# Seven instead of six quads of a first MLP product as seven half-size products, with relus one addition later

## The chip, the cores and the metric

The kernel runs on one core of a Trainium2 chip. The metric is the device time of one execution in microseconds (us); lower is better. Three runs of the kernel before were timed, and one further execution was profiled.

## The reference, cut to what matters

Block-sparse attention, and behind it a token-mixing and a channel-mixing MLP with residuals:

```python
x  = softmax(masked(q @ k.T / 8)) @ v            # 4 batches, 8 heads, 768 tokens, 64 columns a head
a1 = alpha1 * x + beta1
u  = x + lam * einsum('ts,bsd->btd', w_tok, a1)  # 768 x 768 over the tokens
a2 = alpha2 * u + beta2
ch = maximum(a2 @ w_ch1, 0.0) @ w_ch2            # 512 -> 2048 -> 512
out = u + lam * ch
```

The change lies in `a2 @ w_ch1` of the last batch, batch 3.

## The kernel before

The kernel writes out the order of its work by hand. The first batches' attention is laid out by a table of due times; from then on strings of letters (`W1`, `W2`, `W2L`, `W3`) say which job comes next. A letter takes one job from a list: `f` a job of the first MLP product, `g` one of the second, `S` a sum on VectorE that prepares the second product, `W` a sum of weights for the first, `D` a difference of the first product's inputs. The order of the jobs in the strings is the order in which each engine gets its instructions; each engine works through its own in that order and waits by semaphores. The four strings of `W3` are the end of the kernel, when the attention is nearly done: the third and fourth of them hold nothing but `f`, `S` and `g`.

The hidden layer of 2048 is cut into 16 rows of 128, and the 768 tokens into two halves of 384. A *direct job* (`job_f1`, lines 915 to 927) computes one row for one half of the tokens: four matmuls of 384 columns (L919) over the input's four blocks of 128, accumulated in one bank of PSUM, then a relu on ScalarE (L926) that writes `hts` in bf16.

A *quad* is rows n and n + 8 for both halves: four direct jobs, 16 matmuls. In batch 3 a quad can be done instead by seven products of half the depth (Strassen's scheme in Winograd's form), each two matmuls: 14. This is `job_m(n, m)`, product m of quad n, matmuls at L1016. Products 1, 6, 5 and 3 add up in one bank (of tag `sp` or `op`), products 7 and 4 in another, product 2 is alone (both tag `mm`, which has three banks and is also used by the direct jobs). After products 1, 6 and 5 ScalarE copies the partial sum out (`keep_sum`, L999); after 3 it writes the relu (L1027). After products 2, 7 and 4 VectorE adds the kept partial sum to the bank (L1032) and, in a second instruction, takes the maximum with zero (L1035). Product 4 adds into the bank of product 7, after VectorE's addition has read it. So a quad costs VectorE three additions and three relus.

The products take sums of weight blocks (`job_w`, L974, tile `wsum`, for all quads at once) and differences of the inputs (`job_d`, L989). Before, quads 0 to 5 are done this way (`FS = 6`) and the eight direct jobs of quads 6 and 7 stand between them: `last_f1` gives product m of quad n the place 7n + (0, 4, 6, 8, 10, 12, 16) for m = 1, 6, 2, 5, 7, 3, 4, and puts direct jobs at places 1, 5, 42, 46, 48 and 50; two come at the end.

The second MLP product of batch 3 is done by seven products too (`job_p`, matmuls at L1170, additions at L1180, 256 columns each). Its inputs X1, X2 and two differences are the `S` jobs (`job_s`, L1144): 128x512 for half of the rows, 128x1024 for the last of each three. They read the rows that the relus write. The first job of the second product needs rows 0 to 7 of the first half of the tokens, the second one rows 8 to 15.

Of the kernel before, what the change touches and what calls it, by code (L numbers as in the profile page):

```python
# [13 lines left out]
BF = mybir.dt.bfloat16  # L14
# [6 lines left out]
S = 768  # L21
D = 64
# [4 lines left out]
P = 128  # L27
# [53 lines left out]
]  # L81
W3 = [
# [4 lines left out]
]  # L87
STR = (2, 3)
HN = NH // 2
HC = DM // 2  # L90
FS = 6
WEAVE = W1 + W2 + W2L + W3
ENG = {
    "kT0": 0,
# [154 lines left out]
def kernel(  # L249
# [16 lines left out]
    nc = tc.nc  # L266
# [22 lines left out]
    ap_ = ctx.enter_context(tc.tile_pool(name="attn", bufs=1))  # L289
# [4 lines left out]
    def ptile(shape, dt, name):  # L294
        return pp.tile(shape, dt, name=name, tag=name)
# [72 lines left out]
    for n, src in enumerate((moe_lam, moe_alpha1, moe_beta1)):  # L368
# [10 lines left out]
        out=identb[:],  # L379
# [33 lines left out]
    for o in (slice(0, 4), slice(4, NT)):  # L413
# [4 lines left out]
        out=eqt,  # L418
        in0=sampi[0:NBLK, 0 : 2 * NR : 2]
        .unsqueeze(2)  # L420
        .broadcast_to([NBLK, NR, NBLK]),
        in1=eqt,
        op=ALU.is_equal,
# [8 lines left out]
        out=mbs[0:NBLK, :],  # L432
        in0=mbm[0:NBLK, :],
        scalar1=1.0,
# [26 lines left out]
    def sp_tile():  # L461
        return psum.tile([P, 2, 512], FP, name="sp", tag="sp", bufs=2)
# [6 lines left out]
    def mm_tile(shape=(P, DM), dt=FP):  # L469
        return psum.tile(list(shape), dt, name="mm", tag="mm", bufs=3)  # L470

    def op_tile(shape):
        phase["op"] += 1
        if phase["first"] and phase["op"] % 2 == 0:
            return mm_tile(shape)
        return psum.tile(shape, FP, name="op", tag="op", bufs=1)
# [246 lines left out]
    rest = ptile([P, P], FP, "rest")  # L723
# [85 lines left out]
    did = set()  # L809
# [101 lines left out]
    def h_row(b, c, n):  # L911
        if (b, c) not in hts:
            hts[(b, c)] = ap_.tile([P, NH, QC], BF, name="hts", tag="hts", bufs=2)
        return hts[(b, c)][:, n, :]
# [14 lines left out]
    wsum, usum = [], []  # L929
# [19 lines left out]
        7: (3, 3),  # L949
    }  # L950

    def w_of(name, ks, n=slice(0, FS)):
        if isinstance(name, int):
            return wsum[0][:, name - 1, ks, n.start * P : n.stop * P]
        r, c = int(name[0]) - 1, int(name[1]) - 1
        at = slice((HN * r + n.start) * P, (HN * r + n.stop) * P)
        return w1b[:, 2 * c + ks.start : 2 * c + ks.stop, at]

    def u_of(name, ks):
        if isinstance(name, int):  # L960
            t = usum[0][:, name - 1].rearrange("p (k c) -> p k c", k=2)
            return t[:, ks]
        r, c = int(name[0]) - 1, int(name[1]) - 1
        return uTs[B - 1][:, 2 * r + ks.start : 2 * r + ks.stop, ts(c, QC)]

    def job_w(n, ks):
        if not wsum:
            wsum.append(
                ap_.tile([P, 4, 2, FS * P], BF, name="wsum", tag="x_sb", bufs=3)
            )  # L970
        a, b, op = WSUM[n]
        for name in (a, b):
            assert isinstance(name, str) or ("W", name, ks.start) in did
        nc.vector.tensor_tensor(  # L974
            out=w_of(n, ks), in0=w_of(a, ks), in1=w_of(b, ks), op=op
        )
        did.update(("W", n, k) for k in range(ks.start, ks.stop))

    def job_d(n, ks):
        if not usum:  # L980
            usum.append(ap_.tile([P, 4, S], BF, name="uT", tag="uT", bufs=2))
        a, b, op = USUM[n]
        for name in (a, b):
            for k in range(ks.start, ks.stop):
                if isinstance(name, int):
                    assert ("D", name, k) in did
                else:
                    assert ("u", 2 * int(name[0]) - 2 + k) in did
        nc.vector.tensor_tensor(  # L989
            out=u_of(n, ks), in0=u_of(a, ks), in1=u_of(b, ks), op=op  # L990
        )
        did.update(("D", n, k) for k in range(ks.start, ks.stop))
# [3 lines left out]
    def keep_sum(n, name):  # L996
        tag = {1: "kr", 6: ("a1pp128", "ubf")[n % 2], 5: "vr"}[name]
        t = ap_.tile([P, QC], FP, name="part", tag=tag, bufs=2)
        nc.scalar.copy(t[:], chain[(n, 1)][:, 0:QC])  # L999
        chain[(n, "s", name)] = t  # L1000

    def job_m(n, m):
        b = B - 1
        if m == 1 and n % 3 < 2:
            chain[(n, 1)] = sp_tile()[:, 0]
        elif m == 1:
            chain[(n, 1)] = op_tile([P, DM])[:]
        elif m in (2, 7):
            chain[(n, m)] = mm_tile()[:]
        ps = chain[(n, {2: 2, 7: 7, 4: 7}.get(m, 1))]  # L1010
        w, u = PROD1[m]
        for k in range(2):
            ks = slice(k, k + 1)
            assert isinstance(w, str) or ("W", w, k) in did
            assert isinstance(u, str) or ("D", u, k) in did
            nc.tensor.matmul(  # L1016
                ps[:, 0:QC],
                w_of(w, ks, slice(n, n + 1))[:, 0],
                u_of(u, ks)[:, 0],
                start=(m in (1, 2, 7) and k == 0),  # L1020
                stop=(k == 1),
                skip_group_check=True,
            )
        if m in (1, 6, 5):
            keep_sum(n, m)
        elif m == 3:
            nc.scalar.activation(h_row(b, 1, n), ps[:, 0:QC], AF.Relu)  # L1027
            did.add(("f", b, 1, n))
        else:
            part, c, row = {2: (1, 0, n), 7: (5, 1, HN + n), 4: (6, 0, HN + n)}[m]  # L1030
            h = h_row(b, c, row)
            nc.vector.tensor_tensor(  # L1032
                out=h, in0=ps[:, 0:QC], in1=chain[(n, "s", part)][:], op=ALU.add
            )
            nc.vector.tensor_scalar_max(out=h, in0=h, scalar1=0.0)  # L1035
            did.add(("f", b, c, row))

    def last_f1():
        at = {1: 0, 6: 4, 2: 6, 5: 8, 7: 10, 3: 12, 4: 16}
        slot = {7 * n + k: (n, m) for n in range(FS) for m, k in at.items()}  # L1040
        rest = [(c, r + n) for c in range(2) for n in range(FS, HN) for r in (0, HN)]
        jobs = []
        for k in range(max(slot) + 1):
            if k in slot:
                jobs.append(slot[k])
            elif rest and k in (1, 5, 42, 46, 48, 50):
                jobs.append((B - 1,) + rest.pop(0))
        return jobs + [(B - 1,) + j for j in rest]

# [63 lines left out]
    xs = {}  # L1113

    def a_of(b, t, name, r=slice(0, HN)):
        if name in ("X1", "X2"):
            return xs[(b, t, name)][:, r]
        c, half = {"11": (0, 0), "12": (0, 1), "21": (1, 0), "22": (1, 1)}[name]
        return hts[(b, c)][:, HN * half + r.start : HN * half + r.stop, ts(t, P)]
# [7 lines left out]

    def job_s(b, t, n, r=slice(0, HN)):
        dst, a, c, op = SOP[n]
        rows = range(r.start, r.stop)  # L1130
        for name in (a, c):
            if name[0] == "X":
                assert all(("S", b, t, int(name[1]), m) in did for m in rows)
            else:
                h, half = divmod(int(name) - 11, 10)
                assert all(("f", b, h, HN * half + m) in did for m in rows)
        if n == 3:
            assert all(("S", b, t, 1, m) in did for m in rows)
        if n == 4:
            assert (b, t, 2) in did  # L1140
        if dst[0] == "X" and (b, t, dst) not in xs:
            tag, bufs = ("eT", 6) if b == B - 1 else ("xs", 4)
            xs[(b, t, dst)] = ap_.tile([P, HN, P], BF, name="xs", tag=tag, bufs=bufs)
        nc.vector.tensor_tensor(  # L1144
            out=a_of(b, t, dst, r), in0=a_of(b, t, a, r), in1=a_of(b, t, c, r), op=op
        )
        did.update(("S", b, t, n, m) for m in rows)
# [116 lines left out]
    todo = {"f": [], "g": [], "t": [], "S": []}  # L1264
# [52 lines left out]
    for m in (32, 64):  # L1317
        nc.gpsimd.tensor_tensor(
            out=pick[0:96],
            in0=identb[0:96, 0:12] if m == 32 else pick[0:96],  # L1320
            in1=identb[0:96, m : m + 12],
            op=ALU.add,
# [137 lines left out]
    def token(t, p):  # L1460
# [31 lines left out]
            todo[t].pop(0)()  # L1492

    halves = [slice(0, 1), slice(1, 2)]
    todo["W"] = [lambda n=n, k=k: job_w(n, k) for n in (1, 3, 2, 4) for k in halves]
    todo["D"] = [lambda: job_d(1, slice(0, 2))] + [
        lambda n=n, k=k: job_d(n, k) for k in halves[::-1] for n in (2, 3, 4)
    ]
    todo["A"] = [lambda t=t, n=n: job_t(*t, n) for t in T_ORDER for n in range(0, HN, 2)]
# [32 lines left out]
```

## Time and profile before

| | |
|---|---|
| median of 3 runs | 298.61 us (298.60 to 298.87) |
| the profiled execution | 298.76 us, span 297.1 us |
| TensorE matmul (PE), share of the span | 98% |
| VectorE (DVE) | 80% |
| ScalarE (ACT) | 73% |
| first matmul of batch 3's seven products | at 255.34 us |
| first matmul of its second product | at 274.91 us |

In rows of the timeline the first number is the start in us from the span's start, the second the duration; then follow engine, line, operation, what is written and read, the shape, and how many instructions are merged in the row. A merged row's duration is from the start of its first to the end of its last. A bracket at the end gives the idle time before it and what ended it. PE is TensorE, PEld its weight load. A row of the chain of waits has start, duration, engine, tile and line. In the table of stretches each engine has its busy us and, in brackets, its instructions, and the granted clock follows.

### The profile page before, as it was taken

What the parts mean: (1) busy time and instruction counts of PE and PEld (TensorE: products, weight loads), DVE (VectorE), ACT (ScalarE), POOL (GpSimd) and SP (SyncE); (2) the same over time, 40 slices, a digit from 0 to 9 for tenths busy, and PEclk for the clock granted to TensorE, in tenths of its full rate; (3) what the DMA queues carried; (4) which work ended last, traced back from release to release, by engine and by line L of the source; (5) the groups of instructions that cost most, each with busy time, mean ns of one, the idle gap of its engine ahead of it and who ended that gap; (6) DMA issues with size and microseconds to landing.
All of it is one profiled execution on the core that took longest, in us unless ns stands there. A gap on an engine that the chain in (4) does not pass through costs nothing.

```text
span 297.1 us, 7554 instructions
## 1 busy us (share of the span) xinstructions
PE 289.7 (98%) x3082; PEld 193.5 (65%) x3101; DVE 237.8 (80%) x485; ACT 217.1 (73%) x324; POOL 109.8 (37%) x149
## 2 busy tenths in 40 slices
PE   8999999999999999999999999999999999999995
PEld 3688888665567565565576466556576679665884
DVE  4988899995678796977878777895956899799774
ACT  4999999998899963999779581999869744576000
POOL 8997978632443710355323340335320300000000
PEclk9999999999999999999999999999999999999999
DMA  6999999992392995729955767745520211400032
GB/s 182 184 199 186 192 171 187 171 123 44 95 147 55 112 203 84 118 65 119 125 96 73 124 110 146 103 92 69 70 62 17 38 38 29 141 1 3 0 141 73
DMA packets 57274, 31.09 MB, mean 105 GB/s; under 512 B 37204, under 2 KB 54016, under 8 KB 57240
## 3 DMA queue, kind: packets, MB, share of 16 engines
q0 software_dynamic: 16752, 14.22, 34.4%
q1 hardware_dynamic: 40020, 15.92, 29.3%
q8 instruction: 24, 0.39, 0.6%
q10 hardware_dynamic: 468, 0.47, 0.5%
q14 instruction: 10, 0.08, 0.1%
HBM read 29.75 MB, written 6.29 MB: 121 GB/s over the span
## 4 chain that ended last, share of the span: by engine, by line
PE 84%; DVE 6%; DMA 4%; ACT 3%; issue 1%; POOL 1%; SPq 0%; POOLq 0%
PE mm L919 18%; PE mm L1058 13%; PE sp L601 10%; PE mm L846 8%; PE op L671 7%; PE mm L1170 5%; PE sp L1170 4%; PE mm L601 3%; DVE eT L636 3%; PE mm L822 3%; PE op L648 2%; DMA vr<-in_v_dram 2%; ACT eT L619 2%; PE mm L1016 2%; PE sp L1016 2%; DMA uraw<-ubf 2%
## 5 line engine op out<-in xcount | busy, mean ns | idle before, releaser
L619 ACT ACTIVATE eT<-sp,expb 128x1024 f16<-128x1024 f32 x111 | 118.4, 1120 | 2.1 <-PE sp L601 1.4
L636 DVE TENSOR_TENSOR eT<-eT,mask 128x1024 f16<-128x1024 f16 x99 | 80.6, 843 | 13.5 <-ACT eT L619 13.3
L919 PE MATMUL mm<-uT,w1b 128*128 128x384 bf16 x416 | 76.8, 326 | 0.4 <-ACT hts L926 0.3
L705 POOL TENSOR_TENSOR a1pp<-x_sb,vbc 128x384 bf16<-128x384 f32 x25 | 28.5, 1138 | 119.0 <-DVE x_sb L689 84.7
L619 ACT ACTIVATE eT<-mm,expb 128x512 f16<-128x512 f32 x66 | 41.7, 685 | 26.5 <-PE mm L601 26.3
L926 ACT ACTIVATE hts<-mm 128x384 bf16<-128x384 f32 x104 | 49.1, 502 | 13.3 <-PE mm L919 12.4
L919 PEld LDWEIGHTS <-w1b 128*128 128x128 bf16 x416 | 38.7, 98 | 26.4 <-issue 2.9
L1058 PE MATMUL mm<-w2b,hts 128*128 128x512 bf16 x205 | 52.2, 379 | 0.9 <-issue 0.2
L671 PEld LDWEIGHTS <-eT 128*128 128x128 f16 x792 | 29.8, 98 | 8.8 <-issue 1.7
L1058 PEld LDWEIGHTS <-hts 128*128 128x128 bf16 x224 | 19.8, 98 | 22.3 <-issue 3.9
L671 PE MATMUL op<-vext,eT 128*128 128x65 f16 x792 | 32.1, 194 | 0.4 <-DVE x_sb L689 0.3
L601 PE MATMUL sp<-qTs,kTs 88*128 88x512 bf16 (+1 forms) x120 | 26.9, 325 | 1.2 <-ACT eT L619 0.7
L706 POOL TENSOR_TENSOR a1pp<-a1pp,vbc 128x384 bf16<-128x384 bf16 x25 | 26.7, 1069 | 2.0
L846 PE MATMUL mm<-a1pp,wtokT 128*128 128x256 bf16 x216 | 25.9, 273 | 0.1
L846 PEld LDWEIGHTS <-wtokT 128*128 128x128 bf16 x216 | 20.6, 98 | 5.6 <-issue 1.8
L1170 PEld LDWEIGHTS <-hts 128*128 128x128 bf16 x208 | 19.5, 98 | 3.0 <-issue 0.3
L858 DVE TENSOR_TENSOR x_sb<-x_sb,mm 128x512 f32<-128x512 f32 x18 | 12.3, 686 | 9.9 <-PE mm L846 9.8
L601 PE MATMUL sp<-qhT,khT 64*128 64x256 bf16 (+1 forms) x176 | 19.8, 322 | 0.0
L601 PEld LDWEIGHTS <-khT 64*128 64x128 bf16 x264 | 10.6, 94 | 12.7 <-issue 9.2
L648 PEld LDWEIGHTS <-eT 128*128 128x128 f16 x360 | 14.9, 97 | 3.8 <-issue 0.3
L689 DVE TENSOR_TENSOR x_sb<-op,rcp 128x384 f32<-128x384 f32 x28 | 15.6, 558 | 1.0
L1067 DVE TENSOR_TENSOR x_sb<-x_sb,mm 128x512 f32<-128x512 f32 x14 | 9.6, 686 | 8.2 <-PE mm L1058 6.7
(135 smaller groups left out, 376.9 us busy)
## 6 DMA issues: line engine op xcount, KB each, us to landing
out_dram<-x_sb SPq DMA_DIRECT2D x23, 256.0 KB
qpad<-in_q_dram POOLq DMA_DIRECT2D x15, 192.0 KB, 4.6
kr<-in_k_dram POOLq DMA_DIRECT2D x15, 192.0 KB, 5.3
vr<-in_v_dram POOLq DMA_DIRECT2D x15, 192.0 KB, 6.3
w1b<-in_moe_w_ch_dram POOLq DMA_DIRECT2D x4, 512.0 KB, 9.2
w2b<-in_moe_w_ch_dram POOLq DMA_DIRECT2D x4, 512.0 KB, 7.7
hts<-in_moe_w_tok_dram POOLq DMA_DIRECT2D x2, 576.0 KB, 8.7
x_sb<-in_k_dram ACTq DMA_DIRECT2D x2, 192.0 KB
```

Of the source, the lines that this page charges most:

```text
L601: nc.tensor.matmul(sp[jj][:, dst], lhsT, rhs, start=True, stop=True, skip_group_check=True,)
L619: nc.scalar.activation(dst, at, AF.Exp, bias=expb[:], scale=SCALE)
L636: nc.vector.tensor_mul(out=e, in0=e, in1=keep)
L648: nc.tensor.matmul(op[0][:, o, :], ets[u][:, jj, h * QB + n * P : h * QB + n * P + P], vexts[i % NVB][:, w, 2 * jp + jj, :], start=op[1] == 0,
L671: nc.tensor.matmul(op[0][:, o, :], ets[u][:, jj, h * QB + n * P : h * QB + n * P + P], vexts[i % NVB][:, w, 2 * jp + jj, :], start=op[1] == 0,
L705: eng.tensor_tensor(out=dst, in0=x_sbs[b][:, :, cols], in1=bc[0], op=ALU.mult)
L706: eng.tensor_tensor(out=dst, in0=dst, in1=bc[1], op=ALU.add)
L846: nc.tensor.matmul(ps[:, o], wtokT[:, os_, ts(2 * n + o, P)], a1pps[i][:, os_, :], start=(os_ == 0 and o == 0), stop=(os_ == NT - 1 and o ...
L919: nc.tensor.matmul(ps[:, 0:QC], w1b[:, dk, ts(n, P)], uTs[b][:, dk, ts(c, QC)], start=(dk == 0), stop=(dk == 3),)
L926: nc.scalar.activation(h_row(b, c, n), ps[:, 0:QC], AF.Relu)
L1058: nc.tensor.matmul(ps[:], ht[:, nk, ts(o % 3, P)], w2b[:, nk, :], start=(nk == 0), stop=(nk == NH - 1),)
L1170: nc.tensor.matmul(ps, a_of(b, t, a)[:, r], b_rows(m, r)[:, 0, cols], start=(start and r == 0), stop=(r == HN - 1), skip_group_check=True,)
```

## The change

`FS` becomes 7: quad 6 is done by seven products too, and only quad 7 has direct jobs. The weight sums of quad 6 have a tile of their own from the pool of tag `xs`; they are four instructions more (128x256), and four letters `W` at the end of the first string of `W3` place them behind the last differences `D`. In the third string three `f` are added and the `S` are placed anew. Direct jobs stand at places 1, 5, 49 and 53. VectorE's relu after a product is not issued behind its own addition but behind the next one (`raw`, `relu_late`); an `S` job issues it first if it is still due.

```diff
 W3 = [
-    "a p p p g s g g T S T S T S S S d g g U g v g D g D D g D g D g D D",
+    "a p p p g s g g T S T S T S S S d g g U g v g D g D D g D g D g D D W W W W",
     "f f f f f f f f f f f f f f f f f f f f f",
-    "f f f f f f f f f f f f f f f S f f S f f f S S f f S f f S S f f S f f f S f",
+    "f f f f f f f f f f f f f f f f f f S f f S f f S f f S f S f f S f S f f S f f S",
     "S S g S g S g g g S S g S g S g g g S S g S g g g g g S g g g g g",
 ]
-FS = 6
+FS = 7
+FW = 6
...
-    def w_of(name, ks, n=slice(0, FS)):
+    def w_of(name, ks, n):
         if isinstance(name, int):
-            return wsum[0][:, name - 1, ks, n.start * P : n.stop * P]
+            at = n.start // FW
+            return wsum[at][:, name - 1, ks, (n.start - FW * at) * P : (n.stop - FW * at) * P]
...
-    def job_w(n, ks):
-        if not wsum:
-            wsum.append(
-                ap_.tile([P, 4, 2, FS * P], BF, name="wsum", tag="x_sb", bufs=3)
-            )
+    def job_w(n, ks, cs):
+        at = cs.start // FW
+        if len(wsum) == at:
+            tag, bufs = (("x_sb", 3), ("xs", 4))[at]
+            shape = [P, 4, 2, (cs.stop - cs.start) * P]
+            wsum.append(ap_.tile(shape, BF, name="wsum", tag=tag, bufs=bufs))
...
+    raw = []
+
+    def relu_late():
+        while raw:
+            h, name = raw.pop()
+            nc.vector.tensor_scalar_max(out=h, in0=h, scalar1=0.0)
+            did.add(name)
+
...
             nc.vector.tensor_tensor(
                 out=h, in0=ps[:, 0:QC], in1=chain[(n, "s", part)][:], op=ALU.add
             )
-            nc.vector.tensor_scalar_max(out=h, in0=h, scalar1=0.0)
-            did.add(("f", b, c, row))
+            relu_late()
+            raw.append((h, ("f", b, c, row)))
...
-            elif rest and k in (1, 5, 42, 46, 48, 50):
+            elif rest and k in (1, 5, 49, 53):
...
     def job_s(b, t, n, r=slice(0, HN)):
         dst, a, c, op = SOP[n]
+        relu_late()
...
-    todo["W"] = [lambda n=n, k=k: job_w(n, k) for n in (1, 3, 2, 4) for k in halves]
+    both = slice(0, 2)
+    todo["W"] = [
+        lambda n=n, k=k: job_w(n, k, slice(0, FW)) for n in (1, 3, 2, 4) for k in halves
+    ] + [lambda n=n: job_w(n, both, slice(FW, FS)) for n in (1, 3, 2, 4)]
```

In the order that results, TensorE has two matmuls fewer, and all jobs up to place 41 of `last_f1` stand as before, but that the first two direct jobs are now of quad 7. From there on TensorE's jobs are 6.1, 5.5, 4.4, 5.7, 6.6, 5.3, 6.2, a direct job, 6.5, 5.4, 6.7, a direct job, 6.3 and 6.4, where 6.4 is product 4 of quad 6.

More of the change, by code (lines that the diff above doesn't have):

```diff
@@ L964, in u_of @@
         return uTs[B - 1][:, 2 * r + ks.start : 2 * r + ks.stop, ts(c, QC)]
-    def job_w(n, ks):
-        if not wsum:
-            wsum.append(
-                ap_.tile([P, 4, 2, FS * P], BF, name="wsum", tag="x_sb", bufs=3)
-            )
+    def job_w(n, ks, cs):
[4 more added lines that the diff above has]
+            wsum.append(ap_.tile(shape, BF, name="wsum", tag=tag, bufs=bufs))
         a, b, op = WSUM[n]
         for name in (a, b):
-            assert isinstance(name, str) or ("W", name, ks.start) in did
+            for k in range(ks.start, ks.stop):
+                assert isinstance(name, str) or ("W", name, k, at) in did
         nc.vector.tensor_tensor(
-            out=w_of(n, ks), in0=w_of(a, ks), in1=w_of(b, ks), op=op
+            out=w_of(n, ks, cs), in0=w_of(a, ks, cs), in1=w_of(b, ks, cs), op=op
         )
-        did.update(("W", n, k) for k in range(ks.start, ks.stop))
+        did.update(("W", n, k, at) for k in range(ks.start, ks.stop))
     def job_d(n, ks):
@@ L1013, in job_m @@
             ks = slice(k, k + 1)
-            assert isinstance(w, str) or ("W", w, k) in did
+            assert isinstance(w, str) or ("W", w, k, n // FW) in did
             assert isinstance(u, str) or ("D", u, k) in did
@@ L1494 @@
     halves = [slice(0, 1), slice(1, 2)]
-    todo["W"] = [lambda n=n, k=k: job_w(n, k) for n in (1, 3, 2, 4) for k in halves]
-    todo["D"] = [lambda: job_d(1, slice(0, 2))] + [
+    both = slice(0, 2)
+    todo["W"] = [
+        lambda n=n, k=k: job_w(n, k, slice(0, FW)) for n in (1, 3, 2, 4) for k in halves
+    ] + [lambda n=n: job_w(n, both, slice(FW, FS)) for n in (1, 3, 2, 4)]
+    todo["D"] = [lambda: job_d(1, both)] + [
         lambda n=n, k=k: job_d(n, k) for k in halves[::-1] for n in (2, 3, 4)
```

1 row of the table W3 is left out of this document.

## The prediction

> **What bounds the kernel now.** I read the page first, then the busy time by stretches, then the timeline of the stretch that the change touches, then the chain that ended last.
>
> ```profile
> span 297.1 us, 7554 instructions
> PE 289.7 (98%) x3082; PEld 193.5 (65%) x3101; DVE 237.8 (80%) x485; ACT 217.1 (73%) x324; POOL 109.8 (37%) x149
> core 0: us, PE busy (x) PEld busy (x) DVE busy (x) ACT busy (x) POOL busy (x), PEclk, DMA share, GB/s
> 260.00:270.00 10.00, 10.00 (x63) 6.00 (x62) 9.46 (x27) 7.40 (x18) 0.00 (x0) 1.00 0.01 2
> ```
>
> The page says that TensorE bounds the whole: 98%. The stretch from 260 to 270 us, in the middle of batch 3's first product, says something narrower. TensorE is full, at a granted clock of 1.00, but VectorE is busy for 9.46 of 10 us. A change that trades matmuls for VectorE work there spends what hardly exists. I write 6.4 for product 4 of quad 6. The timeline gives the pace of both engines:
>
> ```profile
> 260.95 0.56 DVE L1032 TENSOR_TENSOR hts<-mm,part 128x384 bf16<-128x384 f32 x1
> 261.54 0.26 DVE L1035 TENSOR_SCALAR hts<-hts 128x384 bf16<-128x384 bf16 x1
> 261.72 0.55 DVE L1032 TENSOR_TENSOR hts<-mm,part 128x384 bf16<-128x384 f32 x1
> ...
> 262.05 0.49 PE L1016 MATMUL sp<-uT,w1b 128*128 128x384 bf16 x2
> 264.32 0.49 PE L1016 MATMUL sp<-uT,w1b 128*128 128x384 bf16 x2
> ```
>
> The two TensorE rows are 3.1 and 4.1, the first products of two quads that follow each other: 14 matmuls in 2.27 us, 0.162 each. The VectorE rows are an addition, its relu 0.59 us later (0.03 after the addition ended, so it waited for it), and the next addition 0.18 after that (0.08 before the relu ended, since those two are independent). One addition and its relu so cost 0.76 us, three of them per quad 2.28. The two engines are level: 2.27 against 2.28. What then ended the time of TensorE at the stage's end:
>
> ```profile
> 270.01 0.74 PE mm L1016 x4
> 270.75 0.67 PE mm L919 x4
> 271.45 0.50 ACT hts L926
> 271.99 1.46 PE mm L919 x8
> ...
> 271.25 0.49 PE L1016 MATMUL op<-uT,wsum 128*128 128x384 bf16 x2
> ```
>
> The chain leaves TensorE once: a direct job waited for ScalarE's relu to free its bank, 0.42 us (by the timeline's last row the two matmuls in front began at 271.25, so its own could have followed at 271.57, and began at 271.99; the relu ended at 271.95, so a bank is passed on in about 0.05). After that TensorE runs without a pause into the second product.
>
> **The change part by part.** *TensorE.* Quad 6's four direct jobs are 16 matmuls of 384 columns, its seven products are 14: two fewer, 2 x 0.162 = 0.32 us, if TensorE stays the bound. The 0.42 us wait goes too, since that direct job is gone. ScalarE loses four relus of direct jobs and gains three copies of partial sums and one relu: as many instructions of about the same size, on an engine that is busy for 7.40 of 10 us; I cost it at nothing.
>
> *The four weight sums (128x256).* They stand on VectorE between the last difference of u and the first addition.
>
> ```profile
> 255.88 0.62 DVE L989 TENSOR_TENSOR uT<-uT 128x384 bf16<-128x384 bf16 x2
> 257.96 0.56 DVE L1032 TENSOR_TENSOR hts<-mm,part 128x384 bf16<-128x384 f32 x1 [1.46 <-PE mm L1016]
> ...
> 252.72 1.04 PE L1170 MATMUL sp<-qTs,xs 128*128 128x256 bf16 x8
> ```
>
> VectorE is idle there for 1.46 us, from 256.50 to 257.96. No row has this size: half of the pair of 128x384 is 0.31, a 128x512 of the same kind 0.42 (below), a whole relu 0.26. I take 0.26, nearest to smaller work; four are 1.0 us and fit. At 0.42 they are 1.7 and delay the first addition by 0.2, which VectorE makes up in the next quads, where it will have time over. Their buffer, one of the four of xs, has no reader left: the last matmuls on an X1 or X2 of batch 2 are those of 252.72. Cost at the end: none by either bound.
>
> *Each relu one addition later.* Between additions the relu no longer waits for the addition before it. A following independent instruction starts 0.08 before the end of the one in front, and that holds for work out of PSUM too:
>
> ```profile
> 252.04 0.42 DVE L1180 TENSOR_TENSOR x_sb<-x_sb,sp 128x256 f32<-128x256 f32 x1
> 252.38 0.55 DVE L989 TENSOR_TENSOR uT<-uT 128x768 bf16<-128x768 bf16 x1
> ```
>
> 0.34 us from start to start for a duration of 0.42. So an addition followed by somebody else's relu takes 0.555 - 0.08 = 0.475, against 0.59 now, and the pair 0.475 + 0.18 = 0.655; three per quad are 1.97 us, 0.3 under TensorE's 2.27. In quads 0 to 3 this saves nothing, because TensorE sets their pace. And the relu is flushed at every sum that prepares the second product (L1144): where such a sum comes right after an addition, the relu follows its own addition as before.
>
> *The end of the stage.* This decides. The sums of L1144 must come out of VectorE in this stage too:
>
> ```profile
> L1032 DVE TENSOR_TENSOR hts<-mm,part 128x384 bf16<-128x384 f32 x18 | 9.9, 552 | 1.9 <-PE mm L1016 1.5 <-ACT part L999 0.3
> L1035 DVE TENSOR_SCALAR hts<-hts 128x384 bf16<-128x384 bf16 x18 | 4.7, 260 | 0.6
> L1144 DVE TENSOR_TENSOR xs<-xs,hts 128x512 bf16<-128x512 bf16 x3 | 1.3, 418 | 0.0
> ...
> 269.15 0.26 DVE L1035 TENSOR_SCALAR hts<-hts 128x384 bf16<-128x384 bf16 x1
> 269.32 0.75 DVE L1144 TENSOR_TENSOR xs<-hts 128x512 bf16<-128x512 bf16 x2
> 270.00 0.55 DVE L1032 TENSOR_TENSOR hts<-mm,part 128x384 bf16<-128x384 f32 x1
> ```
>
> Two sums take 0.68 to the next addition, 0.34 each. Before, six direct jobs stand at the end of the stage: 24 matmuls, 3.9 us of TensorE that ask nothing of VectorE. Now there are two, and three additions with three relus more. The order of the changed kernel on VectorE from addition 3.4 on is: 3.4, relu, 4.7, relu, 5.2, two relus, two sums, 4.4, 5.7, two relus, two sums, 6.2, its relu, two sums, 5.4, its relu, a sum, 6.7, its relu, a sum, 6.4, its relu. Up to 3.4 the jobs of TensorE are the same as before, so the matmuls of 3.4 stay where they are:
>
> ```profile
> 267.25 0.49 PE L1016 MATMUL mm<-uT,w1b 128*128 128x384 bf16 x2
> ...
> 274.91 1.04 PE L1170 MATMUL sp<-w2b,hts 128*128 128x256 bf16 x8
> 275.78 1.04 PE L1170 MATMUL mm<-w2b,hts 128*128 128x256 bf16 x8
> ```
>
> They end at 267.74 and the addition starts at about 267.77. From there VectorE does not pause: five additions followed by something independent, 5 x 0.475 = 2.38; four followed by their own relu (6.2, 5.4, 6.7, 6.4), 4 x 0.58 = 2.32; nine relus at 0.18 = 1.62; eight sums at 0.34 = 2.72. Together 9.04: the relu of 6.4 starts at 276.81 and ends at 277.07.
>
> TensorE meets this queue twice. Product 4 of a quad adds into the bank of product 7, so 6.4 waits until addition 6.7 has read it. Counted back from 276.81, addition 6.7 runs from 275.13 to 275.68, and 6.4's matmuls start near 275.7. Unhindered they would start near 273.9 (274.91 less the 0.42, less 0.32 saved, less their own 0.32): new idle time of about 1.8 us, most of it in one piece ahead of 6.4, behind which the whole second product is queued. The next product but one (the second with 256 columns, 275.78 before) reads row 14 of the first half, which the relu of 6.4 writes; it starts at 277.07 + 0.05 = 277.12. That is 277.12 - 275.78 = **+1.34 us**. The saved 0.32 and the vanished 0.42 are inside this, used up by the wait. From there the second product keeps its order and TensorE its pace; its sums come on VectorE 1.3 us later, as all of it does.
>
> The profiled execution took 298.76 us, 1.66 more than its span, and the median is 298.61, so I add to the median: 298.61 + 1.34 = **299.9 us**.
>
> **The rivals.** *The late relus bring nothing.* The rows speak against it (0.75 for two independent sums of 0.42 each). If an addition holds the engine for 0.58 whatever follows, VectorE is behind from the fourth addition on, as it is now: 260.95 + 17 x 0.76 + 8 x 0.34 = 276.59 for addition 6.4, its relu ends at 277.43, the second product goes on at 277.48: +1.70, 300.3 us. The Trainium skill, page "VectorE: DVE Perf Modes", section "The DRAIN you can't avoid", states this as a rule: the next operation does not start until the pipe is empty, and chaining without semaphores does not skip it; it adds that an operation that isn't held starts earlier. The overlap of 0.08 in the rows is on the side of that addition.
>
> *TensorE stays the bound.* Then VectorE would have to finish the relu of 6.4 about 2.1 us earlier than I count: the second product would start 0.32 + 0.42 = 0.74 earlier, near 274.2, and the time is 297.9, or 298.3 if only the matmuls are saved. For it speaks that TensorE is 98% busy and that quads 0 to 3 gain a slack of 0.3 us each on VectorE. Against it: that slack comes before the sums may start, so it cannot be used for them. The point from which it decides is the sum of 9.04 us being under about 7.0.
>
> *In between.* If the nine additions, nine relus and eight sums each cost 0.03 us less than taken, the wait shrinks by 0.8 and the time is 299.2; at 0.05 less it is 298.6, no change.
>
> **How the numbers follow.** About 0.2%, 0.6 us, is what a measurement of this kernel can tell from no change. VectorE as the new bound with late relus at +1.34: 0.77. The same without their help, +1.70: 0.12. In between and within 0.6 us: 0.05. TensorE still the bound, faster: 0.06. So slower 0.89, same 0.05, faster 0.06. The range goes from 299.2 (each term 0.03 us less) to 300.5 (the first rival and 0.2 for terms that are larger than taken).
>
> **What would show it.** In the profile after: a TensorE pause of about 1.5 us or more ahead of the last product 4, with a VectorE addition as the releaser, and VectorE without idle time from about 268 to 277 us. The first product of the second stage starts about 1.1 us later than 274.91. Additions in quads 1 to 3 have relus of the job before right behind them, 0.475 later, and idle time after them. The four weight sums lie inside 256.4 to 257.9. I am wrong if TensorE has no pause over 0.5 us there, or if VectorE shows idle time after 268.

## The result, and the profile after

| | before | after |
|---|---|---|
| median | 298.69 us (19 runs, 298.21 to 299.14) | 299.54 us (19 runs, 299.02 to 300.77) |
| profiled execution | 298.76 us, span 297.1 | 300.77 us, span 299.0 |

The changed kernel is slower: the ratio is 1.003, with an interval of 1.0022 to 1.0038, or 0.85 us from median to median (0.7 to 1.1 by the interval). 299.9 was forecast, with a range of 299.2 to 300.5.

The profiled execution of after is the slowest of its 19 runs. Part of its surplus lies ahead of the change: batch 3's first product begins at 256.29 us, and at 255.34 before, although the instructions up to there are the same in the same order; the other traces of this study begin between 255.00 and 255.87. So I do not compare times on the scales of two traces, but the time from that first matmul. First the page of after:

```profile
span 299.0 us, 7563 instructions
PE 290.0 (97%) x3080; PEld 193.2 (65%) x3099; DVE 240.1 (80%) x495; ACT 217.0 (73%) x324; POOL 109.7 (37%) x149
```

Two matmuls fewer (their weight loads, PEld, go from 3101 to 3099; the PE counts of these two traces lack some 19 records each, which other traces have), ten VectorE instructions more (four weight sums, three additions, three relus), as many on ScalarE. TensorE's share falls although its work hardly shrinks: it waits. Where is shown by TensorE's timeline of after, from the start of the stage to the second product:

```profile
256.29 0.49 PE L1028 MATMUL sp<-uT,w1b 128*128 128x384 bf16 x2
...
273.07 0.49 PE L1028 MATMUL mm<-uT,w1b 128*128 128x384 bf16 x2
273.49 0.48 PE L1028 MATMUL mm<-uT,wsum 128*128 128x384 bf16 x2
274.04 0.81 PE L920 MATMUL mm<-uT,w1b 128*128 128x384 bf16 x4
274.69 0.49 PE L1028 MATMUL sp<-uT,wsum 128*128 128x384 bf16 x2
276.56 0.48 PE L1028 MATMUL mm<-uT,w1b 128*128 128x384 bf16 x2 [1.39 <-DVE hts L1044]
276.89 1.03 PE L1183 MATMUL sp<-w2b,hts 128*128 128x256 bf16 x8
277.76 1.04 PE L1183 MATMUL mm<-w2b,hts 128*128 128x256 bf16 x8
```

The last product of the last quad, 6.4, waits 1.39 us after the end of 6.3, with VectorE's addition (L1044 now) as the releaser. From the stage's first matmul to the second product's first it took 274.91 - 255.34 = 19.57 us before, and 276.89 - 256.29 = 20.60 now: +1.03. From there to the last addition of the kernel both take 18.66 us (293.57 - 274.91 and 295.55 - 276.89). The whole difference is in this stage. It can be added up from start to start, with two matmuls at 0.32: 1.55 us are lost ahead of 6.4 (6.3 begins at 274.69), 0.22 ahead of the direct job at 274.04 and 0.09 ahead of 6.7 (273.49), together 1.86. Before lost 0.42 there and another 0.08 (269.85 to 270.26 for two matmuls). With the two matmuls saved, 1.86 - 0.50 - 0.32 = 1.04. What 6.4 waits for, on VectorE:

```profile
268.72 0.56 DVE L1044 TENSOR_TENSOR hts<-mm,part 128x384 bf16<-128x384 f32 x1 [0.25 <-PE mm L1028]
269.20 0.25 DVE L1011 TENSOR_SCALAR hts<-hts 128x384 bf16<-128x384 bf16 x1
269.36 0.55 DVE L1044 TENSOR_TENSOR hts<-mm,part 128x384 bf16<-128x384 f32 x1
...
270.83 0.75 DVE L1157 TENSOR_TENSOR xs<-hts 128x512 bf16<-128x512 bf16 x2
271.50 1.01 DVE L1044 TENSOR_TENSOR hts<-mm,part 128x384 bf16<-128x384 f32 x2
...
275.63 0.42 DVE L1157 TENSOR_TENSOR hts<-hts 128x512 bf16<-128x512 bf16 x1
275.96 0.55 DVE L1044 TENSOR_TENSOR hts<-mm,part 128x384 bf16<-128x384 f32 x1
276.55 0.26 DVE L1011 TENSOR_SCALAR hts<-hts 128x384 bf16<-128x384 bf16 x1
276.72 0.42 DVE L1157 TENSOR_TENSOR hts<-hts 128x512 bf16<-128x512 bf16 x1
277.09 0.56 DVE L1044 TENSOR_TENSOR hts<-mm,part 128x384 bf16<-128x384 f32 x1
277.68 0.26 DVE L1011 TENSOR_SCALAR hts<-hts 128x384 bf16<-128x384 bf16 x1
```

268.72 is addition 3.4, the last with idle time before it. Behind it VectorE works without a pause until addition 6.7 (275.96 to 276.51), 0.05 us before 6.4 starts. Seven sums for the second product (L1157) stand between 3.4 and 6.7.

### The profile page after: what moved, and what is told of

The parts are those of the page before. It is cut to its first block, busy times and chain, and to the rows that moved or that the text cites. A ratio compares the mean times of both kernels' runs of the same rounds, so it can differ in the third digit from the quotient of the medians.

```text
span 299.0 us, 7563 instructions
## 1 busy us (share of the span) xinstructions
PE 290.0 (97%) x3080; PEld 193.2 (65%) x3099; DVE 240.1 (80%) x495; ACT 217.0 (73%) x324; POOL 109.7 (37%) x149
## 4 chain that ended last, share of the span: by engine, by line
PE 80%; DVE 8%; DMA 6%; ACT 3%; issue 1%; POOL 1%; ACTq 0%; SPq 0%; POOLq 0%
PE mm L920 20%; PE mm L1070 14%; PE sp L602 9%; PE mm L847 8%; PE op L672 8%; PE mm L1183 5%; PE sp L1183 4%; PE mm L602 3%; DMA kr<-in_k_dram 3%; ACT eT L620 2%; PE op L649 2%; PE sp L1028 2%; PE mm L1028 2%; DVE eT L637 2%; DMA uraw<-ubf 1%
## 5 line engine op out<-in xcount | busy, mean ns | idle before, releaser
L920 PE MATMUL mm<-uT,w1b 128*128 128x384 bf16 x400 | 73.9, 326 | 0.2
L927 ACT ACTIVATE hts<-mm 128x384 bf16<-128x384 f32 x100 | 47.1, 502 | 12.1 <-PE mm L920 11.4
L920 PEld LDWEIGHTS <-w1b 128*128 128x128 bf16 x400 | 37.2, 98 | 25.1 <-issue 2.7
```

The lines of the kernel that those rows point to most:

```text
L920: nc.tensor.matmul(ps[:, 0:QC], w1b[:, dk, ts(n, P)], uTs[b][:, dk, ts(c, QC)], start=(dk == 0), stop=(dk == 3),)
L927: nc.scalar.activation(h_row(b, c, n), ps[:, 0:QC], AF.Relu)
```

## The experiments

All kernels below were run against the kernel before. For each I give the ratio's interval in us against before (298.7 to 298.8), and from its trace the time from the stage's first matmul to the kernel's last addition, with the difference to before's 38.23 (293.57 - 255.34). After has 39.26, +1.03.

| kernel | quads, relu, sums | us against before | trace, us |
|---|---|---|---|
| after | 7, late, as given | +0.7 to +1.1 | 39.26 (+1.03) |
| e1 | 6, late, as before | -0.3 to +0.2 | 38.17 (-0.06) |
| e2 | 7, at once, as given | +1.3 to +2.1 | 39.74 (+1.51) |
| e3 | 7, late, moved | -1.1 to -0.4 | 37.30 (-0.93) |
| e4 | as after, weight sums twice | +0.9 to +1.6 | 39.27 (+1.04) |
| e5 | 6, at once, moved | -1.0 to -0.1 | 37.62 (-0.61) |
| e6 | 7, at once, moved as e3 | -0.4 to +0.3 | 38.28 (+0.05) |
| e7 | 7, late, moved otherwise | -1.7 to -0.7 | 37.29 (-0.94) |
| e8 | as after, direct jobs at the end | -0.2 to +0.5 | 38.57 (+0.34) |

**e1, the late relu alone.** The kernel before with this edit only; the list `raw`, `relu_late` and its call in `job_s` come with it, as in the change:

```diff
-            nc.vector.tensor_scalar_max(out=h, in0=h, scalar1=0.0)
-            did.add(("f", b, c, row))
+            relu_late()
+            raw.append((h, ("f", b, c, row)))
```

> The kernel before with one part of the change alone: each relu of VectorE one addition later, six quads as before. Theory (TensorE sets the pace up to the end of quad 4; VectorE's queue matters only from there): VectorE's chain gets shorter by about 0.1 us per pair, but TensorE was not waiting for it; only the bank waits at the end shrink. 0 to 0.1 us faster than before (298.6, within noise). Rival (VectorE with 2.28 us per quad bounds six quads already): 18 pairs x 0.1 = up to 1.8 us, at least 0.5 us faster.

298.52 us, ratio 0.9999 (0.9990 to 1.0008). VectorE's queue is shorter, as its timeline shows: after the second addition the relu starts 0.48 later, no longer 0.59, and VectorE waits for TensorE before the fourth.

```profile
258.87 0.56 DVE L1040 TENSOR_TENSOR hts<-mm,part 128x384 bf16<-128x384 f32 x1 [0.59 <-ACT part L999]
259.35 0.25 DVE L1007 TENSOR_SCALAR hts<-hts 128x384 bf16<-128x384 bf16 x1
...
260.71 0.56 DVE L1040 TENSOR_TENSOR hts<-mm,part 128x384 bf16<-128x384 f32 x1 [0.25 <-PE mm L1024]
```

The end does not come earlier. With six quads VectorE is level with TensorE, but it does not set the end; the rival falls.

**e2, the changed kernel without the late relu.**

```diff
-            relu_late()
-            raw.append((h, ("f", b, c, row)))
+            nc.vector.tensor_scalar_max(out=h, in0=h, scalar1=0.0)
+            did.add(("f", b, c, row))
```

> The changed kernel, with each relu right behind its own addition again. Theory: VectorE is then behind from the fourth addition on (0.76 us a pair), the last product 4 starts about 0.5 us later than in the changed kernel: +0.4 to +0.6 us against it, +1.3 to +1.6 us against before (300.0 to 300.3). Rival (the late relus bring nothing, an addition holds VectorE until its pipe is empty): the same time as the changed kernel, +0.85 us against before.

300.21 us, ratio 1.0058 (1.0045 to 1.0071): slower than after, whose interval ends at 1.0038. TensorE's timeline:

```profile
255.00 0.49 PE L1028 MATMUL sp<-uT,w1b 128*128 128x384 bf16 x2
...
273.22 0.81 PE L920 MATMUL mm<-uT,w1b 128*128 128x384 bf16 x4 [0.32 <-DVE hts L1044]
...
275.75 0.48 PE L1028 MATMUL mm<-uT,w1b 128*128 128x384 bf16 x2 [1.39 <-DVE hts L1044]
276.07 1.04 PE L1183 MATMUL sp<-w2b,hts 128*128 128x256 bf16 x8
```

The wait ahead of 6.4 has the same length, but 6.4 begins 20.75 us after the stage's first matmul, in after 20.27: 0.48 later, because the jobs ahead of it have to wait for VectorE too (the row of 273.22). So with the sums where the change puts them the late relu is worth half a microsecond with seven quads, and nothing that shows with six: it counts where VectorE sets the end.

**e3, the sums moved.** Same instructions as after, in another order on VectorE:

```diff
-    "f f f f f f f f f f f f f f f f f f S f f S f f S f f S f S f f S f S f f S f f S",
-    "S S g S g S g g g S S g S g S g g g S S g S g g g g g S g g g g g",
+    "f f f f f f f f f f f S f f f f f f f f S f f f f f f f S f f f S f f S f",
+    "S S g g S S S S S g g g S g S g g S g S g S g S S g S g g g g g g S g g g",
```

> The changed kernel with the same instructions, but the S jobs (sums for the second product) placed elsewhere in the third and fourth strings: one after the 11th f of the third string, one after the 19th, one after the 26th, two among the last six, the others among the g of the fourth, so that no long row of sums stands ahead of the last additions. Theory (the loss is VectorE's queue ahead of addition 6.7): the wait ahead of the last product 4 falls from 1.4 us to under 0.3 us, and the time is 0.8 to 1.0 us below before (297.7 to 297.9). Rival (the seventh quad itself is too much for VectorE, wherever the sums stand): the wait moves into the second product, +0.3 us or more against before.

297.79 us, ratio 0.9974 (0.9962 to 0.9986): faster than before, by 0.8 us in the middle.

```profile
255.60 0.49 PE L1028 MATMUL sp<-uT,w1b 128*128 128x384 bf16 x2
...
273.69 0.49 PE L1028 MATMUL sp<-uT,wsum 128*128 128x384 bf16 x2
274.01 0.49 PE L1028 MATMUL mm<-uT,w1b 128*128 128x384 bf16 x2
274.34 1.04 PE L1183 MATMUL sp<-w2b,hts 128*128 128x256 bf16 x8
...
270.00:275.00 5.00, 5.00 (x35) 3.18 (x34) 4.93 (x17) 3.17 (x8) 0.00 (x0) 1.00 0.02 5
275.00:280.00 5.00, 5.00 (x48) 4.44 (x46) 4.86 (x14) 0.00 (x0) 0.00 (x0) 1.00 0.00 0
...
267.89 0.43 DVE L1157 TENSOR_TENSOR xs<-hts 128x512 bf16<-128x512 bf16 x1
...
272.42 0.42 DVE L1157 TENSOR_TENSOR xs<-hts 128x512 bf16<-128x512 bf16 x1
272.91 1.02 DVE L1044 TENSOR_TENSOR hts<-mm,part 128x384 bf16<-128x384 f32 x2
273.85 0.42 DVE L1011 TENSOR_SCALAR hts<-hts 128x384 bf16<-128x384 bf16 x2
274.19 0.75 DVE L1157 TENSOR_TENSOR xs<-xs,hts 128x512 bf16<-128x512 bf16 x2
```

6.4 (274.01) follows 6.3 (273.69) without a wait. The stretches say how: TensorE is busy for all of 270 to 280 us while VectorE is as full as in after (4.93 and 4.86 us in the two stretches, 4.97 and 4.86 in after; TensorE had 4.93 and 3.61 there). It does the same work. Additions 5.4 and 6.7 are the row of 272.91, and only three sums stand ahead of 6.7 (at 267.89, before addition 3.4, at 270.15 and at 272.42) instead of seven. The others now lie behind it, most of them beside the second product's first jobs, which do not need them. The rival, that a seventh quad is too much for VectorE in any order, falls.

**e4, the weight sums twice.** Each of the four new instructions is issued twice (with four more letters `W` in the first string).

```diff
-    ] + [lambda n=n: job_w(n, both, slice(FW, FS)) for n in (1, 3, 2, 4)]
+    ] + [lambda n=n: job_w(n, both, slice(FW, FS)) for n in (1, 1, 3, 3, 2, 2, 4, 4)]
```

> The changed kernel with each of the four new weight sums issued twice (eight 128x256 instructions, about 0.9 us of VectorE more between the last difference and the first addition). Theory (VectorE has idle time in quads 1 to 4 and makes it up): the first addition about 0.4 us later, the time as the changed kernel within 0.1 us (+0.85 us against before). Rival (VectorE's queue is full from the first addition on): +0.4 us more than the changed kernel, +1.25 us against before.

299.78 us, ratio 1.0042 (1.0030 to 1.0054). By the intervals alone this could be as after or 0.4 us above it. The trace decides: the stage from the first matmul to the second product takes 276.48 - 255.87 = 20.61 us, 20.60 in after.

```profile
255.87 0.49 PE L1028 MATMUL sp<-uT,w1b 128*128 128x384 bf16 x2
...
261.48 0.56 DVE L1044 TENSOR_TENSOR hts<-mm,part 128x384 bf16<-128x384 f32 x1 [0.25 <-PE mm L1028]
...
276.15 0.49 PE L1028 MATMUL mm<-uT,w1b 128*128 128x384 bf16 x2 [1.39 <-DVE hts L1044]
276.48 1.04 PE L1183 MATMUL sp<-w2b,hts 128*128 128x256 bf16 x8
```

The first addition comes 0.70 us later than in after (259.19 - 255.87 = 3.32 against 258.91 - 256.29 = 2.62), where 0.4 was expected. Before the fourth, at 261.48, VectorE waits for TensorE again, so the delay has been made up. The weight sums are hidden, and so would twice as many be.

**e5, six quads with the sums moved.** The kernel before, with only this edit:

```diff
-    "f f f f f f f f f f f f f f f S f f S f f f S S f f S f f S S f f S f f f S f",
-    "S S g S g S g g g S S g S g S g g g S S g S g g g g g S g g g g g",
+    "f f f f f f f f f f f f f f f f f f S f f f f f S f f S f f S f S S S S S f",
+    "g S S g g S S g S g S g g g S g g g S g g S g g S g S g g S g g g",
```

> The kernel before (six quads, relu right behind its addition), with only the S jobs placed anew: eighteen f without any, then single ones, five ahead of the last f, the rest among the g. It tells what the place of the sums is worth without the seventh quad. Theory: the waits of TensorE at the stage's end (0.42 us for ScalarE's bank and some 0.2 us for VectorE's) go, 0.5 to 0.7 us below before (298.0 to 298.2), and the seventh quad is worth its two matmuls, 0.3 us, on top in the run with seven quads and the sums moved. Rival (the sums cost before nothing, and all of the gain of the run with moved sums is the seventh quad's): no change against before.

298.20 us, ratio 0.9982 (0.9966 to 0.9997). Its trace is 0.61 us shorter than before's: 0.51 in the stage, where TensorE's waits of 0.42 and 0.08 are gone, and 0.10 in the second product, for which no cause was looked for. e3's trace is 0.93 us shorter: 0.32 us more, which is as much as the two matmuls that the seventh quad saves. By the medians' intervals alone the two can't be told apart.

**e6, e3 with each relu at once.** Edit as in e2.

> Seven quads with the sums moved as in the run that was faster, but each relu right behind its own addition. Theory: VectorE's 0.76 us a pair leave it behind from the fourth addition on, and the last product 4 waits 0.6 to 0.8 us again: about 1.0 us slower than the same with late relus, within 0.3 us of before. Rival (with the sums moved the late relus are no longer needed): as the run with moved sums, 0.8 us below before.

298.87 us, ratio 0.9999 (0.9987 to 1.0010). The wait is back, 0.53 us ahead of 6.4, and in its trace the kernel is 0.98 us slower than e3:

```profile
273.45 0.49 PE L1028 MATMUL sp<-uT,wsum 128*128 128x384 bf16 x2
274.47 0.49 PE L1028 MATMUL mm<-uT,w1b 128*128 128x384 bf16 x2 [0.53 <-DVE hts L1044]
```

From start to start 0.70 us are lost ahead of 6.4, and 0.30 in smaller waits ahead of the jobs before it. To be faster than before, seven quads so need both: the late relus, and sums out of the way.

**e7, a second placement,** with the second direct job at place 9:

```diff
-            elif rest and k in (1, 5, 49, 53):
+            elif rest and k in (1, 9, 49, 53):
...
+    "f f f f f f f f f f f f S f f f f f f f S f f f f f f S f f f f f S f S f",
+    "S S S g S g S S g S g g S g g S S g g S g S g g g S g g S g S g g S g g g",
```

> Seven quads, late relus, sums placed anew a second time and the second direct job at place 9 instead of 5. Theory: TensorE has no wait over 0.1 us left in the stage: 0.85 to 1.1 us below before (297.6 to 297.8), equal to or 0.05 us better than the first placement. Rival (VectorE's queue still ends the stage): as the first placement or worse.

297.82 us, ratio 0.9959 (0.9943 to 0.9975): the interval overlaps that of e3, and the traces differ by 0.01 us. Both beat the two kernels of the change; neither beats the other.

**e8, after with the direct jobs at the end.**

```diff
-            elif rest and k in (1, 5, 49, 53):
+            elif rest and k in (49, 53, 55, 56):
```

> The changed kernel with the sums as it has them, but all four direct jobs at the end (places 49, 53, 55, 56), the last two between products 6.3 and 6.4. Theory (what stands ahead of 6.4 on TensorE covers the wait for addition 6.7): the wait there is covered by two direct jobs, 1.3 us; at the stage's start TensorE waits about 0.65 us more for the input's differences, since the first two direct jobs covered that; in sum 0.6 to 0.8 us below the changed kernel, 0.1 to 0.3 us above before. Rival (VectorE's queue sets the end whatever TensorE does ahead of it): as the changed kernel, +0.85 us against before.

299.12 us, ratio 1.0004 (0.9992 to 1.0016), faster than after, whose interval begins at 1.0022; the trace lies 0.69 us below after's.

```profile
255.63 0.48 ACT L1003 COPY part<-sp 128x384 f32<-128x384 f32 x1 [1.24 <-PE sp L1028]
256.16 0.48 PE L1028 MATMUL sp<-uT,wsum 128*128 128x384 bf16 x2 [0.57 <-ACT part L1003]
...
272.78 1.02 DVE L1044 TENSOR_TENSOR hts<-mm,part 128x384 bf16<-128x384 f32 x2
...
273.38 1.46 PE L920 MATMUL mm<-uT,w1b 128*128 128x384 bf16 x8 [0.19 <-DVE hts L1044]
274.68 0.49 PE L1028 MATMUL mm<-uT,w1b 128*128 128x384 bf16 x2
```

Two direct jobs (x8 at 273.38) now stand where TensorE had waited, and 6.4 follows them at once. At the start 0.57 us are lost, but not to the input's differences, as expected: product 6 begins 0.05 us after ScalarE's copy of product 1's sum has ended (256.11), while the difference that it reads (by the kernel's order the fourth of size 128x384 at L993) had ended at 255.12, and the last two ended only at 256.26, after it had begun. That copy is what the direct job had covered.

This run does not tell the theory from its rival. The letters `S` keep their places, but since two direct jobs no longer come first, each sum falls two products later. Five sums instead of seven stand ahead of addition 6.7, the second in the row of 272.78, and addition 3.4 begins 11.86 us after the stage's first matmul instead of 12.43. So 6.7 ends 18.70 us after it, 20.22 in after: VectorE's queue became shorter too. What the direct jobs ahead of 6.4 are worth by themselves is not shown.

## Why the prediction was right, and where a term was off

**The bound and its place: right.** The forecast was a wait ahead of 6.4 with VectorE's addition as the releaser and VectorE without idle time from addition 3.4 on. Both are in the trace; the pause is 1.39 us by its bracket and 1.55 from start to start, where about 1.5 or more was the sign. TensorE's lost time was put at about 1.8 us, and it is 1.86. And e3 shows that the wait is the cause: with the same instructions and no wait, the loss turns into a gain.

**The start of VectorE's queue: right.** Addition 3.4 was put 267.77 - 255.34 = 12.43 us after the stage's first matmul; it is 268.72 - 256.29 = 12.43.

**The sum of 9.04 us: 0.08 too high.** From addition 3.4 to the start of the relu of 6.4 it is 277.68 - 268.72 = 8.96. Single prices: an addition followed by something independent 0.48 (268.72 to 269.20; 0.475 taken), one after a relu 0.16 (269.20 to 269.36; 0.18 taken), two sums 0.67 (270.83 to 271.50; 0.68 taken).

**The start of 6.4: right within 0.1 us.** Forecast 20.4 us after the first matmul (275.7 - 255.34), measured 20.27.

**The step that was mis-sized: what the second product waits for.** I let its second job start when the relu of 6.4 had ended, and got +1.34. In the trace that job starts at 277.76, right behind the first, while this relu runs until 277.94. Its eight matmuls load one row of `hts` each, and row 14 is the seventh; at 0.11 us a matmul (0.87 for eight, from 276.89 to 277.76) it is wanted near 278.4. The term, 0.23 us in the forecast (the second job 1.34 late, the first 1.1), is zero, and with the 0.08 above it makes the 0.31 us between +1.34 and the +1.03 of the trace. The +1.03 lies in the runs' interval of 0.7 to 1.1; the runs do not explain the 0.18 between it and the medians' 0.85.

**The late relus: right, and the rival wrong.** +1.70 without their help was counted, and e2 has +1.51 in its trace, again with about 0.2 us for the second product's start too much. That e2 is slower than after speaks against the Trainium skill's rule (page "VectorE: DVE Perf Modes", section "The DRAIN you can't avoid") that the next operation does not start until the pipe is empty; the section's addition, that an operation that isn't held starts earlier, fits the rows, 0.48 us from an addition to a relu that doesn't read it against 0.59 to its own. What the page counts as held was not tested here.

**The rival with TensorE as the bound** was wrong for this order of the sums, but not far away: its 297.9 us is what e3 and e7 reach once the sums are moved, and by its two terms: in e3 the stage is 0.83 us shorter than before, 0.32 for the two matmuls and 0.51 for the waits. That VectorE's slack in quads 0 to 3 "cannot be used" for the sums was too strong: e3 puts one ahead of addition 3.4, and three instead of seven ahead of addition 6.7.

**The weight sums: right.** They take 1.01 us, and VectorE still waits 0.53 us for TensorE behind them:

```profile
257.36 0.49 DVE L978 TENSOR_TENSOR wsum<-w1b 128x256 bf16<-128x256 bf16 x2
257.77 0.28 DVE L978 TENSOR_TENSOR wsum<-wsum,w1b 128x256 bf16<-128x256 bf16 x1
258.08 0.29 DVE L978 TENSOR_TENSOR wsum<-w1b,wsum 128x256 bf16<-128x256 bf16 x1
258.91 0.56 DVE L1044 TENSOR_TENSOR hts<-mm,part 128x384 bf16<-128x384 f32 x1 [0.53 <-PE mm L1028]
```

That the profiled execution of after begins the stage 0.95 us later than that of before comes for the most part from one load of input. No instruction up to there differs. But in after TensorE waits 0.73 us for that load, where before's trace has no such wait: the matmuls ahead of it begin at 36.97 and 36.98, these at 38.29 and, in before, at 37.41, 0.88 earlier:

```profile
38.29 0.51 PE L512 MATMUL mm<-ident,kr 128*128 128x128 bf16 x6 [0.73 <-DMA kr<-in_k_dram]
```

What stays open is the rest, and why that load came later.

## What to carry to other kernels

When work is traded between two engines that are level over a stage, add up the queue of the engine that gets more from the last place where it still waited to the instruction that the other engine waits for; the share over the stage hides it. Work that is needed later (here the sums for the next product) must not stand in that queue: moving it turned a loss of 0.9 us into a gain of 0.8 with the same instructions. And when you add up the queue, do not let the consumer wait for a whole tile if it takes the tile row by row.

## What the runs showed that I had not expected

A group of eight matmuls starts before its last operands are written: product 2's matmuls began at 277.76, while one of the rows that they load was still being written until 277.94. In e8 the direct jobs at the stage's start turned out to cover ScalarE's copy of a partial sum, and not the input's differences: without them TensorE waited 0.57 us for that copy. And the place of the direct jobs also sets which sums stand ahead of an addition, because both are counted off in one string of letters; moving two of them took two sums out of VectorE's queue.
